# Chunked attention with a rational MLP: two weight pieces converted on GpSimd instead of ScalarE

## The chip, the cores and the metric

One Trainium2 chip, one core of it. The metric is the device time of one execution in microseconds (us). Before the change it is 855.72 us, the median of three runs.

## The reference

```python
scores = scale * np.matmul(q_c, k_c.transpose(0, 1, 2, 4, 3))      # chunks of 64
attn = np.exp(scores - max);  attn = attn / (sum + 1e-09)
x = (attn @ v_c) laid out as (4608, 512)
h = x @ w_in                                                     # (512, 2048)
P = a[0] + a[1] * h + a[2] * h2 + a[3] * h3
Q = 1.0 + np.abs(b[0]) * np.abs(h) + np.abs(b[1]) * h2
g = P / (Q + 1e-06)
return (g @ w_out).astype(np.float32)                            # (2048, 512)
```

The attention outputs of all heads become the 4608 rows of x. The weights arrive in double precision, the rest of the matrices in single precision.

## The kernel before

The 4608 rows are worked in 18 blocks of 256 rows. For each block the attention is made (scores, exponential, sums, the product with v) and split into a high and a low part, `xhi` and `xlo`. Then follow four stages of 512 columns of w_in each: the product `ph` with the weights' high and low parts (`wi_hi`, `wi_lo`), a chain of elementwise steps that makes the rational function (tiles A, B and C), and the product of its high and low parts (`ghi`, `glo`) with w_out (tile `wo`), gathered in `po`.

The first four blocks run while the weights still arrive. Their order is written out by hand in the string START; every word of it is one step, emitted to its engine at that point, and each engine works its own queue strictly in that order. A step is a letter and a number: a piece of the weights (0 to 15), or a stage of a block. What waits for what is found from the tiles that are read and written, including a wait for a buffer that is used again.

A piece of weights is a raw tile of 128 x 1024 double words. It goes through these steps:

- `w` loads it (a DMA from SP's queue; there are three raw buffers in turn).
- `o` or `oa` shifts its low word down: `o` on VectorE as an integer shift, `oa` on ScalarE as a scale and a bias on the upper half of the low word, converted to an integer (line 172).
- `s` scales the high word on ScalarE (line 176).
- `j` joins both words to a single-precision number on VectorE (line 180), and so needs `o`/`oa` and `s`.
- `h` rounds it to the high part on ScalarE (line 183), and so needs `j`.
- `d` or `dp` makes the low part as the difference, on VectorE or on GpSimd (line 190), needs `h`, and sets the raw buffer free.

Pieces 7 and 11 are pieces of w_in. Piece 7 is the second half of the third stage's columns, piece 11 the second half of the fourth's. In the rows their raw tiles are raw_364 (piece 7) and raw_493 (piece 11); raw_334 is piece 9, a piece of w_out.

Steps of the elementwise chain that stand near: `a`, `b`, `c` (lines 361, 365, 369) read `ph` on ScalarE and write A, B, C; `R` (line 404), `H` (line 396, `ghi`) and line 400 are VectorE's; `G` (line 409) makes `glo` from B and A on VectorE, `Gp` on GpSimd. A and B have two buffers each, so `a3` (the tile A_1_594) takes the buffer that A_0_329 leaves when `Gp0` (glo_0_608) has read it.

Of the kernel before, what the change touches and what calls it, by code (L numbers as in the profile page):

```python
# [13 lines left out]
AF = mybir.ActivationFunctionType  # L14
ALU = mybir.AluOpType
# [53 lines left out]
def tile_chunked_attention_rational_moe(  # L69
# [11 lines left out]
    nc = tc.nc  # L81
    cp = ctx.enter_context(tc.tile_pool(name="cp", bufs=1))
    p2 = ctx.enter_context(tc.tile_pool(name="p2", bufs=2))
# [15 lines left out]
    cst = cp.tile([P, 3], F32, tag="cst", name="cst")  # L99
    a0, a1, a2, a3 = (ab[:, i:i + 1] for i in range(4))  # L100
# [40 lines left out]
    raws, pls = {}, {}  # L141

    def grid(x, j):
        return x.rearrange("p (c f) -> p c f", c=2 if PIECES[j][0] else 4)

    def place(j, hi, lo):
        out, fq, k = PIECES[j]
        if out:
            c = slice(4 * fq + 2 * k, 4 * fq + 2 * k + 2)
            return hi[1][:, c, :], lo[1][:, c, :]  # L150
        f = slice(512 * fq + 256 * k, 512 * fq + 256 * k + 256)
        return hi[0][:, :, f], lo[0][:, :, f]
# [6 lines left out]
    def words(j):  # L159
        low, high = raws[j][:, :, 0], raws[j][:, :, 1]  # L160
        return low, high, high.bitcast(F32)

    def w_dest(j):
        return place(j, (wi_hi, wo_hi), (wi_lo, wo_lo))

    def w_low(j):
        low = words(j)[0]
        nc.vector.tensor_scalar(low, low, 29, None, ALU.logical_shift_right)

    def w_low_act(j):  # L170
        upper = raws[j].bitcast(mybir.dt.uint16).rearrange("p f (w h) -> p f w h", h=2)[:, :, 0, 1]
        nc.scalar.activation(words(j)[0], upper, AF.Identity, bias=cst[:, 2:3], scale=2.0 ** -13)

    def w_scale(j):
        val = words(j)[2]
# [12 lines left out]
    def w_diff(engine, j):  # L188
        hi, lo = w_dest(j)
        engine.tensor_sub(lo, grid(words(j)[2], j), hi.bitcast(F32))  # L190
        raws.pop(j)
# [610 lines left out]
    def fetch_behind(s):  # L802
# [3 lines left out]
    of_step = lambda f: lambda g: f(*steps[g])  # L806
    do = {
        "k": consts, "B": coefficients, "C": newton_coefficients, "D": newton_reciprocal, "q": queries, "v": load_v, "w": w_load,
        "o": w_low, "oa": w_low_act, "s": w_scale, "j": w_join, "h": w_hi,
        "d": lambda j: w_diff(nc.vector, j), "dp": lambda j: w_diff(nc.gpsimd, j), "r": w_rest, "l": w_lo,  # L810
        "S": att_s, "M": att_max, "U": att_sub, "E": att_exp, "n": att_rs, "Np": att_norm,
        "N": lambda n, u=None: att_norm(n, u, nc.vector), "m": lambda k: sums_of(*divmod(k, 14)), "t": fetch_behind,
# [176 lines left out]
```

## Time and profile before

| | before |
|---|---|
| median of 3 runs | 855.72 us (854.72 to 855.99) |
| profiled execution | 852.53 us, its span 850.7 us |
| TensorE (PE) busy | 822.4 us, 97% |
| VectorE (DVE) busy | 755.8 us, 89% |
| ScalarE (ACT) busy | 546.0 us, 64% |
| GpSimd (POOL) busy | 573.5 us, 67% |

The profiled execution is 3.2 us below the median; 1.8 us of its own time lie outside the span. The busy shares are means over the whole span, and they hide the first hundred microseconds, where TensorE is not full and the weights are converted.

### The profile page before, as it was taken

What the parts mean: (1) busy time and instruction counts of PE and PEld (TensorE: products, weight loads), DVE (VectorE), ACT (ScalarE), POOL (GpSimd) and SP (SyncE); (2) the same over time, 40 slices, a digit from 0 to 9 for tenths busy, and PEclk for the clock granted to TensorE, in tenths of its full rate; (3) what the DMA queues carried; (4) which work ended last, traced back from release to release, by engine and by line L of the source; (5) the groups of instructions that cost most, each with busy time, mean ns of one, the idle gap of its engine ahead of it and who ended that gap; (6) DMA issues with size and microseconds to landing.
All of it is one profiled execution on the core that took longest, in us unless ns stands there. A gap on an engine that the chain in (4) does not pass through costs nothing.

```text
span 850.7 us, 21032 instructions
## 1 busy us (share of the span) xinstructions
PE 822.4 (97%) x9054; PEld 813.0 (96%) x9054; DVE 755.8 (89%) x653; ACT 546.0 (64%) x550; POOL 573.5 (67%) x359
## 2 busy tenths in 40 slices
PE   2899899999999999999999999999999999999997
PEld 2799899999999999999999999999999999999997
DVE  6999999979888889998989898889888989888887
ACT  5899866657566666565666566666566666666553
POOL 1323475876777776777867777768776768777771
PEclk9999999999999999999999999999999999999999
DMA  8555332514757677777777776768777777776862
GB/s 330 182 186 220 106 119 76 198 51 159 263 154 223 211 233 235 236 248 230 246 242 248 224 252 212 243 215 253 229 248 236 245 243 229 235 229 189 277 214 73
DMA packets 144380, 179.63 MB, mean 211 GB/s; under 512 B 7584, under 2 KB 130464, under 8 KB 141216
## 3 DMA queue, kind: packets, MB, share of 16 engines
q1 hardware_dynamic: 144128, 178.03, 64.7%
q8 instruction: 71, 1.16, 0.5%
q10 hardware_dynamic: 160, 0.26, 0.1%
q14 instruction: 21, 0.17, 0.1%
HBM read 159.39 MB, written 18.87 MB: 210 GB/s over the span
## 4 chain that ended last, share of the span: by engine, by line
PE 86%; DVE 8%; DMA 3%; issue 2%; SPq 1%; ACT 0%; DVEq 0%; ACTq 0%
PE ph L355 40%; PE acc L624 18%; PE acd L624 13%; PE po L430 8%; PE psx L226 2%; PE pss L226 2%; PE pst L306 2%; DVE raw L180 1%; PE pe L668 1%; DMA wo<-t 1%; DMA raw<-in_w_in 1%; DVE C L385 1%; SPq L752 1%; DVE C L389 1%; DVE ghi L396 1%
## 5 line engine op out<-in xcount | busy, mean ns | idle before, releaser
L355 PE MATMUL ph<-xhi,wi_hi 128*128 128x256 f32 x1156 | 320.4, 278 | 2.2 <-DVE C L501 2.2
L355 PE MATMUL ph<-xhi,wi_lo 128*128 128x256 f32 x1152 | 319.6, 277 | 1.5 <-DVE wi_lo L190 1.5
L355 PE MATMUL ph<-xlo,wi_hi 128*128 128x256 f32 x1152 | 319.6, 277 | 0.0
L355 PEld LDWEIGHTS ph<-xhi,wi_hi 128*128 128x128 f32 x1156 | 218.1, 189 | 3.0 <-issue 2.3
L355 PEld LDWEIGHTS ph<-xhi,wi_lo 128*128 128x128 f32 x1152 | 217.4, 189 | 1.9 <-DVE wi_lo L190 1.9
L355 PEld LDWEIGHTS ph<-xlo,wi_hi 128*128 128x128 f32 x1152 | 217.6, 189 | 0.1
L553 POOL TENSOR_TENSOR slo<-B,shi 128x1024 fp32r<-128x1024 f32 x54 | 131.3, 2432 | 71.3 <-ACT shi L545 70.1
L463 ACT ACTIVATE U<-ph 128x1024 f32<-128x1024 f32 x64 | 65.8, 1030 | 159.9 <-PE ph L355 159.4
L472 DVE SCALAR_TENSOR_TENSOR U<-U,co 128x1024 f32<-128x1024 f32 x64 | 117.2, 1831 | 20.0 <-ACT U L463 20.0
L529 POOL TENSOR_TENSOR B<-C 128x512 f32<-128x512 f32 x54 | 81.6, 1511 | 67.6 <-DVE C L501 67.6
L493 DVE SCALAR_TENSOR_TENSOR U<-U,co,ph 128x1024 f32<-128x1024 f32 x64 | 80.5, 1258 | 42.6 <-ACT ph L489 42.5
L521 POOL TENSOR_TENSOR graw<-C,graw 128x768 fp32r<-128x768 f32 x54 | 100.0, 1852 | 0.7 <-ACT graw L516 0.7
L485 ACT ACTIVATE B<-U,cst,co 128x1024 f32<-128x1024 f32 x64 | 79.8, 1247 | 27.3 <-DVE U L472 26.2
L624 PE MATMUL acc<-wo,graw 128*128 128x256 f32 x648 | 92.6, 278 | 0.0
L489 ACT ACTIVATE ph<-B,co 128x1024 f32<-128x1024 f32 x64 | 71.6, 1119 | 19.1 <-DVE C L480 18.9
L480 DVE SCALAR_TENSOR_TENSOR C<-C,co,ph 128x1024 f32<-128x1024 f32 x64 | 81.8, 1277 | 1.7
L468 ACT ACTIVATE C<-ph,co 128x1024 f32<-128x1024 f32 x64 | 77.0, 1203 | 9.7 <-PE ph L355 6.0
L501 DVE SCALAR_TENSOR_TENSOR C<-C,co,ph 128x1024 f32<-128x1024 f32 x63 | 80.7, 1281 | 2.2
L624 PEld LDWEIGHTS acc<-wo,graw 128*128 128x128 f32 x648 | 81.7, 188 | 0.8
L497 DVE SCALAR_TENSOR_TENSOR ph<-U,ph 128x1024 f32<-128x1024 f32 x64 | 78.5, 1226 | 1.7
L534 POOL TENSOR_TENSOR B<-C,B 128x256 f32<-128x256 f32 x54 | 75.4, 1396 | 4.2
L476 DVE TENSOR_TENSOR C<-C,ph 128x1024 f32<-128x1024 f32 x64 | 77.5, 1211 | 0.2 <-ACT U L463 0.2
(118 smaller groups left out, 1577.8 us busy)
## 6 DMA issues: line engine op xcount, KB each, us to landing
wo<-t SPq DMA_DIRECT2D x106, 768.0 KB, 6.4
wo<-t SPq DMA_DIRECT2D x114, 256.0 KB, 3.4
out<-o SPq DMA_DIRECT2D x68, 128.0 KB, 6.0
raw<-in_w_in SPq DMA_DIRECT2D x8, 1024.0 KB, 5.1
raw<-in_w_out SPq DMA_DIRECT2D x8, 1024.0 KB, 4.8
v<-in_vP SPq DMA_DIRECT2D x24, 256.0 KB, 7.8
qk<-in_qT SPq DMA_DIRECT2D x44, 128.0 KB, 6.6
qk<-in_kT SPq DMA_DIRECT2D x44, 128.0 KB, 6.3
```

Of the source, the lines that this page charges most:

```text
L355: nc.tensor.matmul(ph[:, fi, t], w[:, cc, f], x[:, cc, t], start=(k == 0 and i == 0), stop=(k == len(mm) - 1),)
L472: nc.vector.scalar_tensor_tensor(U, U, c0, U, ALU.add, ALU.mult)
L476: nc.vector.tensor_mul(C, C, h)
L480: nc.vector.scalar_tensor_tensor(C, C, na1, h, ALU.add, ALU.mult)
L485: nc.scalar.activation(ch[key][2], ch[key][1], AF.Ln, bias=cst[:, 0:1], scale=lsc)
L493: nc.vector.scalar_tensor_tensor(V, V, kq, h, ALU.add, ALU.mult)
L497: nc.vector.scalar_tensor_tensor(h, V, 2.0, h, ALU.subtract, ALU.mult)
L501: nc.vector.scalar_tensor_tensor(C, C, na0, h, ALU.add, ALU.mult)
L521: nc.gpsimd.tensor_sub(lo, quads(ch[steps[g]][3])[:, :, 1:4, :], hi.bitcast(F32))
L529: nc.gpsimd.tensor_sub(S[:, 0:2], q[:, 0:1].to_broadcast([P, 2, 2, 128]), q[:, 1:3])
L553: nc.gpsimd.tensor_sub(lo, sbuf[g], hi.bitcast(F32))
L624: nc.tensor.matmul(acc[n][pair][:, bank, col + t.start:col + t.stop], stat, mov[:, t], start=start and k == 0, stop=stop and k == len(part ...
```

## The change

For the pieces 7 and 11 the step `oa` becomes `op`, a GpSimd instruction that multiplies and adds on the same upper halves, and `h` becomes `hp`, a copy on GpSimd. The words stand at the same places of START. No other step is changed.

```diff
-    "... F3:pa w11 s9 Q2 I2 s7 oa7 Z0 R0 p2 J2 P2 j7 z0 s11 g2 h7 F1:p1 f3 "
-    "H2 oa11 a3 d7 oa9 b3 j11 R2 h11 c3 j9 w6 Gp0 h9 Z2 G2 f1 d11 a1 f5:p0 ..."
+    "... F3:pa w11 s9 Q2 I2 s7 op7 Z0 R0 p2 J2 P2 j7 z0 s11 g2 hp7 F1:p1 f3 "
+    "H2 op11 a3 d7 oa9 b3 j11 R2 hp11 c3 j9 w6 Gp0 h9 Z2 G2 f1 d11 a1 f5:p0 ..."
...
+    def upper_half(j):
+        return raws[j].bitcast(mybir.dt.uint16).rearrange("p f (w h) -> p f w h", h=2)[:, :, 0, 1]
+
     def w_low_act(j):
-        upper = raws[j].bitcast(mybir.dt.uint16).rearrange("p f (w h) -> p f w h", h=2)[:, :, 0, 1]
-        nc.scalar.activation(words(j)[0], upper, AF.Identity, bias=cst[:, 2:3], scale=2.0 ** -13)
+        nc.scalar.activation(words(j)[0], upper_half(j), AF.Identity, bias=cst[:, 2:3], scale=2.0 ** -13)
+
+    def w_low_pool(j):
+        nc.gpsimd.tensor_scalar(words(j)[0], upper_half(j), 2.0 ** -13, -4095.5 / 8192.0, ALU.mult, ALU.add)
+
+    def w_hi_pool(j):
+        nc.gpsimd.tensor_copy(w_dest(j)[0], grid(words(j)[2], j))
```

How the queues stand. Line numbers of the changed kernel are 8 higher from line 182 on.

GpSimd's queue before, from the normalisation of block 1 and the low part of piece 8 on:

```order
L296 TENSOR_TENSOR e_258<-e_258,sm_253 128x2x8x64
L190 TENSOR_TENSOR wo<-raw_268,wo 128x1024
L409 TENSOR_TENSOR glo_0_608<-B_0_336,A_0_329 128x1024
L190 TENSOR_TENSOR wo<-raw_334,wo 128x1024
L190 TENSOR_TENSOR wi_lo<-raw_606,wi_hi 128x4x256
```

GpSimd's queue in the changed kernel, from the same place on:

```order
L304 TENSOR_TENSOR e_258<-e_258,sm_253 128x2x8x64
L198 TENSOR_TENSOR wo<-raw_268,wo 128x1024
L177 TENSOR_SCALAR raw_364<-raw_364 128x1024
L180 CAST wi_hi<-raw_364 128x4x256
L177 TENSOR_SCALAR raw_493<-raw_493 128x1024
L180 CAST wi_hi<-raw_493 128x4x256
L417 TENSOR_TENSOR glo_0_608<-B_0_336,A_0_329 128x1024
L198 TENSOR_TENSOR wo<-raw_334,wo 128x1024
```

The four new instructions (op7, hp7, op11, hp11) stand ahead of Gp0, which makes glo_0_608.

ScalarE's queue before, from the scaling of piece 7 on (the brackets name the engines or DMA queues that an instruction waits for):

```order
L176 ACTIVATE raw_364<-raw_364 128x1024 [waits DMAHW2_49,Pool_49]
L172 ACTIVATE raw_364<-raw_364,cst 128x1024
L381 ACTIVATE A_1_459<-A_1_459,cst 128x1024 [waits Activation_49]
L176 ACTIVATE raw_493<-raw_493 128x1024 [waits DMAHW3_49]
L183 CAST wi_hi<-raw_364 128x4x256 [waits DVE_49]
L172 ACTIVATE raw_493<-raw_493,cst 128x1024
L361 ACTIVATE A_1_594<-ph_1_467,ab 128x1024 [waits PE_49,Pool_49]
L172 ACTIVATE raw_334<-raw_334,cst 128x1024
L365 ACTIVATE B_1_598<-ph_1_467 128x1024
L183 CAST wi_hi<-raw_493 128x4x256 [waits DVE_49]
L369 ACTIVATE C_1_603<-ph_1_467,ab 128x1024
```

ScalarE's queue in the changed kernel, from the same place on:

```order
L184 ACTIVATE raw_364<-raw_364 128x1024 [waits DMAHW2_49,Pool_49]
L389 ACTIVATE A_1_459<-A_1_459,cst 128x1024 [waits Activation_49]
L184 ACTIVATE raw_493<-raw_493 128x1024 [waits DMAHW3_49]
L369 ACTIVATE A_1_594<-ph_1_467,ab 128x1024 [waits PE_49,Pool_49]
L174 ACTIVATE raw_334<-raw_334,cst 128x1024
L373 ACTIVATE B_1_598<-ph_1_467 128x1024 [waits DVE_49]
L377 ACTIVATE C_1_603<-ph_1_467,ab 128x1024
L191 CAST wo<-raw_334 128x1024 [waits DVE_49]
```

Four instructions are gone. The wait of A_1_594 (a3) for GpSimd is there before and after; in both programs it is the wait for Gp0. Behind it stands oa9, the shift of piece 9.

VectorE's queue in the changed kernel, from the join of piece 7 on:

```order
L188 SCALAR_TENSOR_TENSOR raw_364<-raw_364 128x1024 [waits DMAHW2_49,Activation_49,Pool_49]
L404 SCALAR_TENSOR_TENSOR ghi_1_539<-C_1_464,ab,A_1_459 128x1024 [waits DVE_49,Activation_49]
L408 SCALAR_TENSOR_TENSOR B_1_461<-B_1_461,ghi_1_539 128x1024 [waits DVE_49]
L198 TENSOR_TENSOR wi_lo<-raw_364,wi_hi 128x4x256 [waits Pool_49]
L188 SCALAR_TENSOR_TENSOR raw_493<-raw_493 128x1024 [waits DMAHW3_49,Activation_49,Pool_49]
L412 SCALAR_TENSOR_TENSOR B_1_461<-C_1_464,ab,B_1_461 128x1024 [waits DVE_49]
L188 SCALAR_TENSOR_TENSOR raw_334<-raw_334 128x1024 [waits DMAHW1_49,Activation_49]
L417 TENSOR_TENSOR glo_1_627<-B_1_461,A_1_459 128x1024 [waits DVE_49]
```

Its order is that of before (the DVE rows of the next section show it). The difference of piece 7 waited for ScalarE and now waits for GpSimd, and the join of piece 11 waits for GpSimd as well. The join of piece 9 (raw_334) waits for ScalarE's oa9, as before.

## Rows read from the trace of the kernel before

**Rows 1.** The page: the span, and the chain that ended last by engine.

```profile
span 850.7 us, 21032 instructions
...
PE 86%; DVE 8%; DMA 3%; issue 2%; SPq 1%; ACT 0%; DVEq 0%; ACTq 0%
```

**Rows 2.** Windows: busy us and instruction counts by engine, granted clock, DMA.

```profile
40.00:100.00 60.00, 56.36 (x529) 55.58 (x529) 59.58 (x53) 54.10 (x58) 23.78 (x9) 0.98 0.52 185
50.00:60.00 10.00, 10.00 (x91) 10.00 (x90) 9.93 (x9) 9.88 (x10) 1.97 (x1) 1.00 0.24 78
```

**Rows 3.** The chain in order of time near 98 us: start, us, what.

```profile
97.50 1.29 DVE C L501
...
98.93 4.59 PE ph L355 x24
...
105.33 2.72 PE ph L355 x24
```

**Rows 4.** Timeline of VectorE, 39 to 66 us: start, duration, instruction.

```profile
39.94 1.22 DVE L180 SCALAR_TENSOR_TENSOR raw<-raw 128x1024 int32<-128x1024 int32 x1
...
48.06 1.28 DVE L404 SCALAR_TENSOR_TENSOR B<-C,ab,B 128x1024 f32<-128x1024 f32 x1
...
51.71 1.35 DVE L180 SCALAR_TENSOR_TENSOR raw<-raw 128x1024 int32<-128x1024 int32 x1
52.98 1.27 DVE L396 SCALAR_TENSOR_TENSOR ghi<-C,ab,A 128x1024 fp32r<-128x1024 f32 x1
54.28 1.23 DVE L400 SCALAR_TENSOR_TENSOR B<-B,ghi 128x1024 f32<-128x1024 f32 x1
55.43 1.22 DVE L190 TENSOR_TENSOR wi_lo<-raw,wi_hi 128x1024 fp32r<-128x1024 f32 x1
56.56 1.22 DVE L180 SCALAR_TENSOR_TENSOR raw<-raw 128x1024 int32<-128x1024 int32 x1
57.70 1.28 DVE L404 SCALAR_TENSOR_TENSOR B<-C,ab,B 128x1024 f32<-128x1024 f32 x1
58.89 1.22 DVE L180 SCALAR_TENSOR_TENSOR raw<-raw 128x1024 int32<-128x1024 int32 x1
...
63.43 2.52 DVE L373 SCALAR_TENSOR_TENSOR B<-B,ab,A 128x1024 f32<-128x1024 f32 x1
```

**Rows 5.** Timeline of ScalarE, 50 to 58 us.

```profile
50.27 1.25 ACT L172 ACTIVATE raw<-raw,cst 128x1024 int32<-128x1024 uint16 x1
...
53.49 1.15 ACT L183 CAST wi_hi<-raw 128x1024 fp32r<-128x1024 f32 x1
...
55.94 1.12 ACT L361 ACTIVATE A<-ph,ab 128x1024 f32<-128x1024 f32 x1
56.96 1.26 ACT L172 ACTIVATE raw<-raw,cst 128x1024 int32<-128x1024 uint16 x1
```

**Rows 6.** Timeline of GpSimd, 40 to 65 us; brackets: idle before, and what ended it.

```profile
40.53 2.95 POOL L190 TENSOR_TENSOR wo<-raw,wo 128x1024 fp32r<-128x1024 f32 x1 [7.39 <-ACT wo L183]
49.49 2.48 POOL L409 TENSOR_TENSOR glo<-B,A 128x1024 fp32r<-128x1024 f32 x1 [6.00 <-DVE B L404]
62.41 2.46 POOL L190 TENSOR_TENSOR wo<-raw,wo 128x1024 fp32r<-128x1024 f32 x1 [10.44 <-ACT wo L183]
```

**Rows 7.** DMA issues between 43 and 44 us: count, size, us to landing.

```profile
raw<-in_w_in SPq DMA_DIRECT2D x1, 1024.0 KB, 4.8
```

**Rows 8.** GpSimd's groups by form: count, busy us, mean ns, idle before.

```profile
L190 POOL TENSOR_TENSOR wi_lo<-raw,wi_hi 128x1024 fp32r<-128x1024 f32 x2 | 4.9, 2443 | 4.7 <-ACT wi_hi L183 4.7
...
masks.py:199 POOL TENSOR_SCALAR_AFFINE_SELECT ident<-ident 128x128 f32<-128x128 f32 x1 | 0.3, 292 | 0.1
masks.py:197 POOL MEMSET ident<- 128x128 f32 x1 | 0.2, 204 | 0.3 <-POOLq L969 0.3
...
L777 POOL MEMSET cst<- 128x1 f32 x1 | 0.1, 98 | 0.0
```

**Rows 9.** Timeline of TensorE: its first wait for VectorE's last step.

```profile
98.93 0.36 PE L355 MATMUL ph<-xhi,wi_hi 128*128 128x256 f32 x1 [2.18 <-DVE C L501]
```

More of the change, by code (lines that the diff above doesn't have):

```diff
@@ L808, in tile_chunked_attention_rational_moe @@
         "k": consts, "B": coefficients, "C": newton_coefficients, "D": newton_reciprocal, "q": queries, "v": load_v, "w": w_load,
-        "o": w_low, "oa": w_low_act, "s": w_scale, "j": w_join, "h": w_hi,
+        "o": w_low, "oa": w_low_act, "op": w_low_pool, "hp": w_hi_pool, "s": w_scale, "j": w_join, "h": w_hi,
         "d": lambda j: w_diff(nc.vector, j), "dp": lambda j: w_diff(nc.gpsimd, j), "r": w_rest, "l": w_lo,
```

4 rows, old and new, of the table START are left out of this document.

## Prediction

> **What bounds the kernel now.** I read the page first. Its chain that ended last is TensorE for 86% of the 850.7 us and VectorE for 8%, about 68 us [rows 1]. A mean like that says nothing about a change at 50 us, so the next view was the chain in order of time. VectorE's last piece in it ends at 98.79 us, TensorE goes on at 98.93, and from there the chain stays with TensorE [rows 3]. TensorE itself stood idle for 2.18 us just then, and what released it was VectorE [rows 9]. So up to about 99 us VectorE sets the time, and behind it TensorE does. The windows say the same: from 40 to 100 us VectorE is busy for 59.58 of 60 us, TensorE for 56.36. Between 50 and 60 us ScalarE is nearly full too, 9.88 of 10, but VectorE with 9.93 is not waiting for it; GpSimd is busy for 1.97 [rows 2].
>
> What follows from this: four instructions fewer on ScalarE give nothing back by themselves, since VectorE's queue has no gap to close. A delay of VectorE before 99 us is passed on to the end in full, as TensorE cannot make it up later.
>
> **What goes and what comes.** ScalarE loses two shifts and two roundings, of 1.25 and 1.15 us in the rows of piece 7 [rows 5], some 4.8 us in all, none of it on the path. GpSimd gains four instructions of 128 x 1024. The trace has no GpSimd instruction with one such input, so I bound one. The two-input kind takes 2443 ns, an upper bound. A memset of 128 elements takes 204 ns and one of a single element 98, which is 0.83 ns an element and 0.95 us for 1024, a lower bound since it reads nothing. The nearest row reads one input and writes one output: the 128x128 select with 292 ns; (292 - 98)/127 is 1.53 ns an element, 1.66 us for 1024 [rows 8]. I take 1.6 us for each, o for a shift and h for a rounding, with 0.95 to 2.45 as bounds. The GPSIMD Engine Reference of the Trainium skill (section 3.1, Elementwise) gives about 1.8 cycles an element at best, by which I estimate 1.54 us; the delay below would be 9.3 instead of 9.5 us.
>
> **The new wait inside VectorE's queue.** The load of piece 7 is issued just after 43.5 us and lands 4.8 us later, near 48.4 [rows 7]. GpSimd is free by then: its low part of piece 8 ends at 43.48 [rows 6]. So op7 is done near 50 to 51.7, before VectorE comes to j7 at 51.71 [rows 4]. No cost there; j7 even loses the 0.13 us by which it was longer than the other joins (1.35 against 1.22), since GpSimd no longer runs glo_0_608 at that time.
>
> From j7 on VectorE's queue is j7, ghi, line 400, d7, j11. Its starts follow at 1.14, 1.30, 1.15 and 1.13 us [rows 4], so j11 would start at 51.71 + 4.72 = 56.43. But d7 now needs hp7, and j11 needs op11 behind hp7 on GpSimd. Can these two hide under VectorE's work? The trace has a row on that. VectorE's line 373 at 63.43 takes 2.52 us, where 1.27 is usual for such an instruction; GpSimd's instruction ended at 62.41 + 2.46 = 64.87, and VectorE's ended 1.08 us behind that [rows 4, 6]. The other way round, GpSimd's instruction at 40.53 took 2.95 us in place of 2.46, while VectorE's join ran until 41.16 [rows 4, 6]. So two SBUF inputs on VectorE and a GpSimd instruction do not run together. The State Buffer page of the Trainium skill (section Who interferes with whom) calls it an exclusive lock, held for the whole instruction, between VectorE with two SBUF inputs and any GpSimd instruction that reads SBUF; by that the delay is 9.5 us, and by overlap 5.3. The rows agree for two-input GpSimd instructions; no row has one with a single input. The instructions ghi, line 400, d7 and j11 have two SBUF inputs each, so I add both GpSimd times to the line: j11 starts at 56.43 + h + o, which is later than before (56.56) by h + o - 0.13 = 3.1 us. Which of the two gets in first does not matter for the sum.
>
> **The longer wait: Gp0 behind hp11.** GpSimd's queue is in order, and Gp0 now stands behind hp11, which needs j11. Gp0 ran at 49.49 before [rows 6]. ScalarE's a3 waits for Gp0 (it takes over its buffer), oa9 stands behind a3 on ScalarE, and VectorE's join of piece 9 needs oa9. Counted from the start of j11: VectorE's next instruction starts at 1.14 and holds the inputs until 1.14 + 1.28 = 2.42 (start and length of the row at 57.70). So hp11 ends at 2.42 + h. Gp0 takes 2.48: 4.90 + h. From a3 to oa9 are 56.96 - 55.94 = 1.02 us, and oa9 takes 1.26 [rows 5]: the join of piece 9 starts at 7.18 + h. Before it was 58.89 - 56.56 = 2.33 behind j11 [rows 4]. The added wait is 4.85 + h, 6.45 us, in which VectorE does nothing. Hand-overs of under 0.1 us each are left out.
>
> **The sum.** h + o - 0.13 + 4.85 + h = 4.72 + 2h + o, with 1.6 us for both 9.5 us. With 0.95 it is 7.6, with 2.45 it is 12.1. After the join of piece 9 each engine finds its queue as before, only later: c3, needed next from ScalarE, comes some 2 us behind oa9, while VectorE has three instructions of 1.2 us to do first. The loads that wait for the raw buffers of pieces 7 and 11 go out 3 and 9 us later, with VectorE. The 9.5 us then reach TensorE at 98.93 and the end. The span becomes 860.2 us, the profiled execution 852.53 + 9.5 = 862.0. That execution lies 3.2 us below the median of 855.72, so for the median I say 855.7 + 9.5 = 865.2 us.
>
> **Rivals.** (1) GpSimd with a single input runs beside VectorE. Then hp7 (52.93 to about 54.7) and op11 are done in time for d7 and j11, which gain 0.13. The hand-over from VectorE to GpSimd was 0.15 us (48.06 + 1.28 to 49.49) [rows 4, 6], so hp11 starts 1.22 + 0.15 behind j11, Gp0 ends at 3.85 + h, the join of piece 9 starts at 6.13 + h, and the delay is 3.67 + h = 5.3 us: 861.0. With h of 0.95 it is 4.6: 860.3. For it: no row has the single-input kind. Against it: the rows above show no kind that went beside. Chance 0.13.
>
> (2) Not slower: Gp0 is done before a3 needs it, at 55.94 [rows 5], and the 4.8 us taken from ScalarE count. With ScalarE ahead, GpSimd's low part of piece 9 at 62.41 would come earlier and no longer hold VectorE at 63.43 (1.25 us), and j7 gains 0.13: 855.7 - 1.4 = 854.3, within 0.2%. It decides if hp11 ends before 55.94 - 2.48 = 53.5. Against it: hp11 needs j11, four instructions behind j7 on VectorE, and j7 starts at 51.71; only a queue that lets Gp0 pass would do it. A kin of it is that the delay is hidden later, but VectorE had 0.42 us idle in all from 40 to 100 us [rows 2]. Both 0.05.
>
> (3) Longer GpSimd instructions: 16-bit input at a stride and the conversion to integers cost more than two float inputs, or TensorE comes back at a lower clock. The 24 matmuls from 98.93 took 4.59 us, those from 105.33 took 2.72 [rows 3], so a restart behind a wait can cost 1.9 us. With 3 us for o and h the delay is 13.7: 869.4, and 871.3 with such a restart. Chance 0.09.
>
> The forecast keeps 0.73.
>
> **Numbers.** Its own range is 855.7 + 7.6 to 855.7 + 12.1, 863.3 to 867.8. The range takes in rival 1 down to 860.3 less the 1 us by which runs of before lie apart, and upward 867.8 and a restart: 859.5 to 869.7. A difference under 0.2%, 1.7 us, is about what a measurement of this kernel cannot tell from none. Slower by more than that are the forecast and the rivals 1 and 3, 0.95; rival 2 is mostly no change, 0.03, and faster with 0.02.
>
> **What the next profile would show.** Gp0 starts behind hp11, past 60 us instead of at 49.49, and a3 on ScalarE shows an idle time of several us, released by GpSimd. VectorE shows two stalls: about 3 us between line 396 and the join of piece 11, partly as longer instructions, and about 6.5 us ahead of the join of piece 9. GpSimd's new instructions take between 0.95 and 2.45 us. VectorE's last piece in the chain ends near 108 instead of 98.79, and behind it all is as before. I am wrong if VectorE's instructions keep their length beside GpSimd's (rival 1), if a3 does not wait, or if the chain finds 9 us again between 68 and 99 us.

## The result and the profile after

The changed kernel takes 861.96 us, median of five runs (861.67 to 865.99); the kernel before, run beside it, 855.72 us, median of five (854.12 to 859.43). The ratio is 1.0068, 95% interval 1.0041 to 1.0095, which is 5.8 us more with 3.5 to 8.1. The medians lie 6.2 us apart. The change makes the kernel slower.

The page of the profile after, its span and its chain by engine, beside [rows 1]:

```profile
span 860.5 us, 21031 instructions
...
PE 83%; DVE 8%; DMA 3%; issue 2%; POOL 2%; ACT 1%; SPq 0%; DVEq 0%; POOLq 0%; ACTq 0%
```

GpSimd and ScalarE were hardly in the chain before; now they hold 2% and 1%. Where, the chain in order of time says (start, us, what):

```profile
60.58 2.08 POOL wi_hi L180
62.66 2.41 POOL glo L417
65.10 1.11 ACT A L369
66.21 1.09 ACT raw L174
67.33 0.04 DVE raw L188
...
105.78 1.29 DVE C L509
107.07 0.14 issue
107.21 4.32 PE ph L363 x24
```

It goes from GpSimd's rounding of piece 11 through Gp0 (line 417) to ScalarE's a3 (line 369) and oa9 (line 174), and to the join of piece 9 on VectorE (line 188). Before, VectorE held this stretch alone. Behind it nothing is new: from the join of piece 9 to the end of VectorE's last step are 107.07 - 67.33 = 39.74 us, and before 98.79 - 58.89 = 39.90 us [rows 3, 4].

The windows (span of the window; busy us and instruction counts of PE, weight loads, DVE, ACT, POOL; granted clock of TensorE; DMA share; GB/s), beside [rows 2]:

```profile
40.00:100.00 60.00, 55.43 (x515) 54.84 (x509) 54.11 (x46) 44.52 (x49) 29.59 (x12) 0.90 0.43 158
50.00:60.00 10.00, 10.00 (x90) 10.00 (x89) 9.93 (x8) 4.28 (x5) 5.60 (x3) 1.00 0.14 57
60.00:70.00 10.00, 5.43 (x47) 5.23 (x46) 4.38 (x5) 4.90 (x5) 4.49 (x2) 0.95 0.28 105
65.00:70.00 5.00, 0.43 (x3) 0.26 (x2) 2.67 (x3) 4.90 (x5) 0.07 (x1) 0.91 0.00 0
70.00:75.00 5.00, 5.00 (x24) 5.00 (x25) 5.00 (x4) 5.00 (x6) 2.73 (x1) 0.50 0.65 215
```

VectorE, full before, is busy for 54.11 of 60 us; the loss lies between 60 and 70 us, where it works for 4.38 of 10. From 50 to 60 us it looks as full as before, 9.93 us, but with 8 instructions in place of 9: a wait inside an instruction counts as busy. Its timeline (start, us, instruction; brackets: idle before, and what ended it), beside [rows 4]:

```profile
52.88 1.22 DVE L188 SCALAR_TENSOR_TENSOR raw<-raw 128x1024 int32<-128x1024 int32 x1
54.02 1.28 DVE L404 SCALAR_TENSOR_TENSOR ghi<-C,ab,A 128x1024 fp32r<-128x1024 f32 x1
55.33 2.02 DVE L408 SCALAR_TENSOR_TENSOR B<-B,ghi 128x1024 f32<-128x1024 f32 x1
57.27 2.11 DVE L198 TENSOR_TENSOR wi_lo<-raw,wi_hi 128x1024 fp32r<-128x1024 f32 x1
59.30 1.22 DVE L188 SCALAR_TENSOR_TENSOR raw<-raw 128x1024 int32<-128x1024 int32 x1
60.44 1.27 DVE L412 SCALAR_TENSOR_TENSOR B<-C,ab,B 128x1024 f32<-128x1024 f32 x1
67.33 1.23 DVE L188 SCALAR_TENSOR_TENSOR raw<-raw 128x1024 int32<-128x1024 int32 x1 [5.62 <-ACT raw L174]
```

The two stalls can be read off. Lines 408 and 198 take 2.02 and 2.11 us in place of 1.23 and 1.22: 0.79 and 0.89 us inside the instruction. Then VectorE stands still for 5.62 us before the join of piece 9. GpSimd's timeline, beside [rows 6]:

```profile
49.53 2.00 POOL L177 TENSOR_SCALAR raw<-raw 128x1024 int32<-128x1024 uint16 x1 [4.89 <-DMA raw<-in_w_in]
54.16 2.10 POOL L180 CAST wi_hi<-raw 128x1024 fp32r<-128x1024 f32 x1 [2.63 <-DVE raw L188]
56.34 1.97 POOL L177 TENSOR_SCALAR raw<-raw 128x1024 int32<-128x1024 uint16 x1
60.58 2.08 POOL L180 CAST wi_hi<-raw 128x1024 fp32r<-128x1024 f32 x1 [2.27 <-DVE raw L188]
62.63 2.44 POOL L417 TENSOR_TENSOR glo<-B,A 128x1024 fp32r<-128x1024 f32 x1
```

Gp0 starts at 62.63 instead of 49.49, behind the rounding of piece 11. The new instructions show some 2 us each, but about half of that is waiting: the rounding at 60.58 ends at 62.66, and VectorE's line 412, which held the inputs, ended at 60.44 + 1.27 = 61.71. From there it took 0.95 us. On ScalarE, a3 shows the wait for Gp0, and oa9 follows it:

```profile
65.10 1.11 ACT L369 ACTIVATE A<-ph,ab 128x1024 f32<-128x1024 f32 x1 [10.82 <-POOL glo L417]
66.11 1.18 ACT L174 ACTIVATE raw<-raw,cst 128x1024 int32<-128x1024 uint16 x1
```

How much later is the kernel behind this stretch? A mark that every kernel has is VectorE's first row maximum of a block. The marks of blocks 1 and 2, before (line 262) and after (line 270):

```profile
23.59 1.23 DVE L262 TENSOR_REDUCE sm<-pss 128x16 f32<-128x1024 f32 x1 [0.40 <-PE pss L226]
77.00 1.22 DVE L262 TENSOR_REDUCE sm<-pss 128x16 f32<-128x1024 f32 x1
...
24.76 1.22 DVE L270 TENSOR_REDUCE sm<-pss 128x16 f32<-128x1024 f32 x1 [0.40 <-PE pss L234]
85.26 1.22 DVE L270 TENSOR_REDUCE sm<-pss 128x16 f32<-128x1024 f32 x1
```

The 1.17 us ahead of block 1 are not the change's: VectorE's first shift waits for the first piece of w_in, and starts at 9.23 instead of 8.06. So between the two marks the change costs 8.26 - 1.17 = 7.09 us. I call this the local cost below. In block 3 the shift is 125.83 - 117.55 = 8.28 us, the same. Further back the two profiled executions drift apart by another 1 to 2 us and together again, and end at 860.5 against 850.7, which a pair of single executions can't put down to the change. Part of the drift shows on TensorE, in the chain after:

```profile
130.43 8.48 PE ph L363 x72
```

That is 117.8 ns a matmul, where before 72 of them take 8.16 us at 122.28, 113.3 ns each. The granted clock is 1.00 in both from 120 to 800 us. Later blocks mostly take the same 44.42 us in both kernels.

### The profile page after: what moved, and what is told of

It is laid out like the page before. It is cut to its first block, busy times and chain, and to the rows that moved or that the text cites. A ratio compares the mean times of both kernels' runs of the same rounds, so it can differ in the third digit from the quotient of the medians.

```text
span 860.5 us, 21031 instructions
## 1 busy us (share of the span) xinstructions
PE 827.2 (96%) x9054; PEld 817.5 (95%) x9054; DVE 760.5 (88%) x653; ACT 541.0 (63%) x546; POOL 582.9 (68%) x363
## 4 chain that ended last, share of the span: by engine, by line
PE 83%; DVE 8%; DMA 3%; issue 2%; POOL 2%; ACT 1%; SPq 0%; DVEq 0%; POOLq 0%; ACTq 0%
PE ph L363 39%; PE acc L632 17%; PE acd L632 13%; PE po L438 6%; PE psx L234 2%; DMA wo<-t 2%; PE pss L234 2%; PE pst L314 2%; DMA raw<-in_w_in 1%; DVE U L480 1%; PE pe L676 1%; DVE raw L188 1%; DVE C L393 1%; DVE B L381 1%; DVE sm L297 1%
## 5 line engine op out<-in xcount | busy, mean ns | idle before, releaser
L480 DVE SCALAR_TENSOR_TENSOR U<-U,co 128x1024 f32<-128x1024 f32 x64 | 120.1, 1876 | 18.5 <-ACT U L471 18.4
```

The lines of the kernel that those rows point to most:

```text
L480: nc.vector.scalar_tensor_tensor(U, U, c0, U, ALU.add, ALU.mult)
```

## The experiments

All were timed in five rounds beside runs of the kernel before on the same chip. The local cost of each is the shift of block 2's mark less that of block 1's, read from one profiled execution. This table has all results; the profiles follow one by one.

| kernel | median, of before | ratio (95%) | as us | local cost, us |
|---|---|---|---|---|
| the change | 861.96, 855.72 | 1.0068 (1.0041 to 1.0095) | 5.8 | 7.09 |
| e1_gp0_early | 860.37, 857.94 | 1.0027 (1.0006 to 1.0048) | 2.3 | 3.78 |
| e2_shift_only | 859.31, 857.94 | 1.0020 (0.9996 to 1.0045) | 1.7 | 2.22 |
| e3_round_only | 864.26, 857.94 | 1.0082 (1.0050 to 1.0113) | 7.0 | 7.16 |
| e4_wait_only | 886.14, 857.94 | 1.0328 (1.0293 to 1.0364) | 28.1 | 6.22 |
| e5_wait_only | 860.65, 856.79 | 1.0057 (1.0032 to 1.0082) | 4.9 | 5.70 |
| e6_six_copies | 861.24, 856.79 | 1.0048 (1.0023 to 1.0073) | 4.1 | 5.19 |
| e7_six_memsets | 856.92, 856.79 | 1.0002 (0.9977 to 1.0027) | 0.2 | -0.15 |
| e8_apart | 853.83, 856.79 | 0.9976 (0.9951 to 1.0002) | -2.1 | -1.72 |

In the profiled executions of five kernels, part of the local cost lies ahead of the join of piece 7 and is not due to what they change. VectorE waits for ScalarE there, for 0.29 us in e1, 0.73 in e3, 0.76 in e4, 0.39 in e5 and 0.75 in e6. In e3, for one, ScalarE itself had first waited 1.75 us for TensorE's `ph`. The profile of before has no such wait.

**Gp0 put ahead.** The changed kernel with Gp0 moved to a place before the first rounding, so that a3 need not wait for hp11:

```diff
-    "... j7 z0 s11 g2 hp7 F1:p1 f3 "
-    "H2 op11 a3 d7 oa9 b3 j11 R2 hp11 c3 j9 w6 Gp0 h9 ..."
+    "... j7 z0 s11 g2 Gp0 hp7 F1:p1 f3 "
+    "H2 op11 a3 d7 oa9 b3 j11 R2 hp11 c3 j9 w6 h9 ..."
```

> The changed kernel with the step Gp0 put ahead of hp7 in GpSimd's queue; nothing else differs. Queue theory (most of the loss is a3 waiting for Gp0 behind hp11): the idle time of ScalarE ahead of a3 that GpSimd ends (10.8 us in the changed kernel) falls under 1.5 us and VectorE's 5.6 us of idle time ahead of the join of piece 9 is gone; what stays is the shared inputs, 1.2 us for j7 behind Gp0, 1.6 for hp7 and op11, 0.95 for hp11: 2.5 to 4 us above before, about 859. Rival (the GpSimd instructions themselves hold VectorE up): the loss stays at 6 us, about 862.

Two rows of VectorE and one of ScalarE from its timelines:

```profile
48.67 2.21 DVE L412 SCALAR_TENSOR_TENSOR B<-C,ab,B 128x1024 f32<-128x1024 f32 x1
...
62.13 2.13 DVE L188 SCALAR_TENSOR_TENSOR raw<-raw 128x1024 int32<-128x1024 int32 x1
...
57.73 1.12 ACT L369 ACTIVATE A<-ph,ab 128x1024 f32<-128x1024 f32 x1 [4.04 <-PE ph L363]
```

The wait is gone: a3 starts at 57.73, released by TensorE and not by GpSimd, and the join of piece 9 at 62.13 has no idle time ahead of it. What is left is the sharing. The join itself takes 2.13 us beside the rounding of piece 11, line 412 takes 2.21 beside the first shift, and from the join of piece 7 (53.24) to that of piece 11 (59.80) are 6.56 us, before 4.85 [rows 4]. Together 0.91 + 0.93 + 1.71 = 3.55 of the local 3.78 us. The sum is near the one expected, but not all of its parts: Gp0 does not hold the join of piece 7 longer than before (1.33 us, before 1.35), and the wait of line 412 beside the first shift was not foreseen. Nearly half of the local cost goes by moving one word.

**The shifts alone**, the rounding left on ScalarE (`hp7` and `hp11` back to `h7` and `h11`):

```diff
-    "... s11 g2 hp7 F1:p1 f3 H2 op11 a3 d7 oa9 b3 j11 R2 hp11 c3 ..."
+    "... s11 g2 h7 F1:p1 f3 H2 op11 a3 d7 oa9 b3 j11 R2 h11 c3 ..."
```

> Only the two shifts on GpSimd, the rounding on ScalarE as before. Queue theory: Gp0 stands behind op11, which needs nothing of VectorE, so Gp0 ends near 54 to 55.5 and a3 hardly waits; Gp0 now meets VectorE's j7 and ghi and costs up to 2.4 us: 0.5 to 2.5 us above before, 856.2 to 858.2. Rival: half of the GpSimd work, half of the loss, 3 us, 858.7, and a3 as late as in the changed kernel.

Two rows of GpSimd and one of VectorE:

```profile
52.17 1.15 POOL L177 TENSOR_SCALAR raw<-raw 128x1024 int32<-128x1024 uint16 x1 [0.63 <-DVE C L393]
53.41 3.31 POOL L417 TENSOR_TENSOR glo<-B,A 128x1024 fp32r<-128x1024 f32 x1
...
54.33 3.47 DVE L404 SCALAR_TENSOR_TENSOR ghi<-C,ab,A 128x1024 fp32r<-128x1024 f32 x1
```

Here the shift of piece 11 runs beside an instruction of VectorE that reads one of its inputs from `ph`, TensorE's output, and takes 1.15 us: the price of a shift alone. Gp0 starts at 53.41, before at 49.49, and now meets `ghi`, which takes 3.47 us in place of 1.28. That is 2.19 of the 2.22 us of the local cost. So the shifts themselves hardly make VectorE wait here (the join of piece 7 takes 1.51 us, before 1.35); they push Gp0 onto another instruction with which it can't share. The timed 1.7 us have an interval that just takes in none. From the join of piece 11 to that of piece 9 are 62.45 - 60.11 = 2.34 us, as before (2.33).

**The rounding alone**, the shifts left on ScalarE:

```diff
-    "... s7 op7 Z0 R0 p2 J2 P2 j7 z0 s11 g2 hp7 F1:p1 f3 H2 op11 a3 ..."
+    "... s7 oa7 Z0 R0 p2 J2 P2 j7 z0 s11 g2 hp7 F1:p1 f3 H2 oa11 a3 ..."
```

> Only the two roundings on GpSimd, the shifts on ScalarE as before. Queue theory: Gp0 stays behind hp11 and so behind the join of piece 11; the wait ahead of the join of piece 9 stays at 5 to 6 us and the shared inputs cost 0.9 less than in the changed kernel: 5.5 to 7 us above before, 861 to 862.5. Rival: half of the GpSimd work, 3 us, 858.7.

One row each of GpSimd, ScalarE and VectorE:

```profile
62.55 2.44 POOL L417 TENSOR_TENSOR glo<-B,A 128x1024 fp32r<-128x1024 f32 x1
...
65.02 1.12 ACT L369 ACTIVATE A<-ph,ab 128x1024 f32<-128x1024 f32 x1 [8.19 <-POOL glo L417]
...
67.24 1.23 DVE L188 SCALAR_TENSOR_TENSOR raw<-raw 128x1024 int32<-128x1024 int32 x1 [5.62 <-ACT raw L174]
```

The rounding alone costs as much as the full change, 7.16 us locally, with the same 5.62 us ahead of the join of piece 9. The 0.9 us that leaving the shifts on ScalarE was expected to save are there: line 198 takes 1.22 us in place of 2.11. But they do not show in the total, since in this execution VectorE lost 0.73 us ahead of the join of piece 7: 0.29 for ScalarE's step `b` and 0.44 for the shift of piece 7 on ScalarE.

**The wait alone, first try.** The kernel before, with one instruction more: GpSimd copies one element of the joined piece 11 ahead of Gp0, so that Gp0 stands behind j11 with no conversion to do. The copied element is read by nobody.

```diff
-    "H2 oa11 a3 d7 oa9 b3 j11 R2 h11 c3 j9 w6 Gp0 ..."
+    "H2 oa11 a3 d7 oa9 b3 j11 R2 x11 h11 c3 j9 w6 Gp0 ..."
+    look = cp.tile([P, 1], F32, tag="look", name="look")
...
+    def w_look(j):
+        nc.gpsimd.tensor_copy(look, words(j)[2][:, 0:1])
```

> The kernel before with one GpSimd copy of a single element per partition, read from the joined piece 11, just ahead of Gp0; shifts and roundings stay on ScalarE. This has the queue's wait without the work. Queue theory: Gp0 starts near 59 instead of 49.5, a3 near 61.6, the join of piece 9 near 63.9 instead of 58.9: 4.5 to 5 us above before, 860.5. Rival: under 0.3 us, 855.7 to 856.

It came out 28 us slower, far from anything expected. The local cost is 6.22 us, so the rest is elsewhere, and two marks far behind show where (block starts on VectorE):

```profile
268.20 1.23 DVE L266 TENSOR_REDUCE sm<-pss 128x16 f32<-128x1024 f32 x1
314.38 1.23 DVE L266 TENSOR_REDUCE sm<-pss 128x16 f32<-128x1024 f32 x1
```

A block takes 46.18 us there, and before 302.43 - 258.01 = 44.42. Every later block is some 1.7 us longer, though not one instruction of them differs. The page shows on which engine:

```profile
PE 852.8 (97%) x9054; PEld 843.2 (95%) x9054; DVE 742.5 (84%) x653; ACT 542.9 (61%) x550; POOL 577.6 (65%) x360
```

TensorE is busy for 852.8 us with the same 9054 matmuls that take 822.4 before; in the later blocks 48 in a row take 5.68 us instead of 5.44 (118.3 ns each instead of 113.3), at a granted clock of 1.00. What does differ is the place of the tiles: the new tile has 4 bytes per partition and moves all tiles made after it. The run can't be used for the wait, and was made again without the new tile.

**The wait alone, second try.** The same copy, written into a filler tile of the kernel that is already there and never read:

```diff
-    cp.tile([P, 48], F32, tag="gap", name="wo_gap")
+    look = cp.tile([P, 48], F32, tag="gap", name="wo_gap")
...
+    def w_look(j):
+        nc.gpsimd.tensor_copy(look[:, 0:1], words(j)[2][:, 0:1])
```

> The wait without the work again: the kernel before with one GpSimd copy of a single element per partition, read from the joined piece 11, ahead of Gp0, now written into the gap that the kernel already has, so that no tile moves (in the run before, a new tile moved all later ones). Queue theory: VectorE's idle time ahead of the join of piece 9 is 4 to 5 us, the steady blocks take the time that they take before, 5 to 6.5 us above before, about 861. Rival (the shared inputs are the loss): under 1.3 us, since one element per partition holds nothing up.

Two rows of GpSimd, two of VectorE:

```profile
59.35 1.18 POOL L175 COPY wo_gap<-raw 128x1 f32<-128x1 f32 x1 [14.73 <-DVE raw L183]
60.48 2.44 POOL L412 TENSOR_TENSOR glo<-B,A 128x1024 fp32r<-128x1024 f32 x1
...
65.18 1.23 DVE L183 SCALAR_TENSOR_TENSOR raw<-raw 128x1024 int32<-128x1024 int32 x1 [4.71 <-ACT raw L172]
...
69.73 3.07 DVE L376 SCALAR_TENSOR_TENSOR B<-B,ab,A 128x1024 f32<-128x1024 f32 x1
```

With no conversion at all, the order of the queue alone costs 4.9 us timed and 5.70 locally. From the join of piece 11 (58.06) to that of piece 9 are 7.12 us, before 2.33: 4.79 us. The prediction's term for this wait, without the rounding, was 4.85. Line 376 takes 3.07 us in place of 2.52, another 0.55, as GpSimd's low part of piece 9 now meets it differently. The rest of the local cost is the wait of 0.39 us ahead of the join of piece 7.

**The sharing alone.** The kernel before with six single-input GpSimd copies of 128 x 1024 behind Gp0, where nothing waits for them, and once with six memsets in the same place. Both write a part of `wo` that later gets its weights, so the result doesn't change; one memset at the start fills the source.

```diff
-    "... c3 j9 w6 Gp0 h9 Z2 ..."
+    "... c3 j9 w6 Gp0 x0 h9 Z2 ..."
...
+    spare = [wo[:, 0, c:c + 2, :].bitcast(F32) for c in (12, 14)]
+    nc.gpsimd.memset(spare[1], 0.0)
...
+        for _ in range(6):
+            nc.gpsimd.tensor_copy(wo[:, 0, 12:14, :], spare[1])
```

With the memsets the last line is `nc.gpsimd.memset(spare[0], 0.0)`.

> The kernel before with six GpSimd copies of 128 x 1024, one input each, behind Gp0, into a part of wo that is written over later; nothing waits for them. If a single-input instruction and two SBUF inputs on VectorE exclude each other, VectorE's instructions between 52 and 65 us grow by about 0.95 us for each copy that meets one: 4 to 5.7 us above before, 860 to 861.5. If they run beside each other: under 0.3 us, 856.

> The same with six memsets of the same size, which read nothing from SBUF. If only reading shares the inputs: VectorE's instructions keep their length, under 0.5 us, 856. If every GpSimd instruction shares them: as the copies, 4 to 5.5 us.

GpSimd and two rows of VectorE with the copies:

```profile
51.92 10.94 POOL L787 CAST wo<-wo 128x1024 fp32r<-128x1024 f32 x6
...
53.96 2.06 DVE L396 SCALAR_TENSOR_TENSOR ghi<-C,ab,A 128x1024 fp32r<-128x1024 f32 x1
...
57.92 2.06 DVE L190 TENSOR_TENSOR wi_lo<-raw,wi_hi 128x1024 fp32r<-128x1024 f32 x1
```

And with the memsets:

```profile
52.91 6.05 POOL L787 MEMSET wo<- 128x1024 f32 x6
...
53.97 1.27 DVE L396 SCALAR_TENSOR_TENSOR ghi<-C,ab,A 128x1024 fp32r<-128x1024 f32 x1
...
56.42 1.22 DVE L190 TENSOR_TENSOR wi_lo<-raw,wi_hi 128x1024 fp32r<-128x1024 f32 x1
```

With copies, VectorE's instructions grow from 1.22 to 1.28 us to about 2.06, and the two engines take turns: from the join of piece 7 to that of piece 9 VectorE needs 63.86 - 52.27 = 11.59 us in place of 58.89 - 51.71 = 7.18. That is 4.41 us for six copies, 0.74 each, less than the 0.95 expected; the rest of the local 5.19 us is the 0.75 us ahead of the join of piece 7. With memsets no instruction of VectorE grows, and the time is that of before. So a GpSimd instruction that reads one input holds up VectorE's two-input instructions, and one that only writes does not. The SBUF — State Buffer page of the Trainium skill (section Who interferes with whom) says just this: two SBUF inputs on VectorE contend with a GpSimd instruction that reads SBUF, not with one that only writes it. The runs agree, with 0.74 us a copy and nothing for a memset.

**Apart.** A try at the reverse: give GpSimd only what it can hide. The kernel before, with the shift of piece 8 (on VectorE until now) on GpSimd, behind the normalisation of block 1, and with line 373 (`Q3`) put behind `P3`, whose instructions read `ph`, so that these stand beside GpSimd's low part of piece 9.

```diff
-    "... s8 o8 Q0 ...  p3 Q3 s6 q2 y2 oa6 b1 P3 dp9 ..."
+    "... s8 op8 Q0 ...  p3 P3 s6 q2 y2 oa6 b1 Q3 dp9 ..."
```

> The kernel before with VectorE's line 373 of the fourth chain behind its line 389, so that GpSimd's low part of piece 9 falls beside instructions that read PSUM, and with the shift of piece 8 on GpSimd in place of VectorE's. If the shared inputs are what holds VectorE up: line 373 takes 1.3 to 1.6 us in place of 2.52, and 0.6 us of VectorE's shift goes: 0.8 to 1.6 us below before, 854.1 to 854.9, which may not stand out of the measurement. Rival: nothing, 855.7.

One row of GpSimd and two of VectorE:

```profile
34.08 2.03 POOL L176 TENSOR_SCALAR raw<-raw 128x1024 int32<-128x1024 uint16 x1
...
35.00 1.21 DVE L389 TENSOR_TENSOR C<-C,ph 128x1024 f32<-128x1024 f32 x1
...
64.99 1.28 DVE L377 SCALAR_TENSOR_TENSOR B<-B,ab,A 128x1024 f32<-128x1024 f32 x1
```

The instruction that took 2.52 us beside GpSimd [rows 4] takes 1.28, since the instructions ahead of it that now run beside GpSimd read `ph`, and keep their length. VectorE's shift of 0.68 us is gone, and the shift on GpSimd holds nobody (the instruction beside it reads `ph`, 1.21 us). Locally this gains 1.72 us, and the median is 853.83 us, the lowest of all kernels here; the ratio of 0.9976 has an interval that just takes in 1.

## Why the prediction was right, point by point

**The bound.** VectorE sets the time up to about 99 us, and a delay there is passed on: shown. The local cost of every kernel but e4, from -1.72 to 7.16 us, lies in the interval of its timed difference. Whether it is passed on in full is less sure: for the six kernels in the table that are slower, e4 aside, the timed difference is smaller than the local cost each time, by 0.2 to 1.5 us. In e1, e3, e5 and e6, 0.3 to 0.8 us of the local cost are the wait ahead of the join of piece 7, which is not due to what they change. Single executions differ by more, among other things in the pace of TensorE (113.3 or 117.8 ns a matmul), so this stays open. That ScalarE's four instructions give nothing back was read from one execution. In e5, with the shift of piece 7 still on ScalarE, ScalarE waited 1.27 us for `ph` and VectorE then 0.39 us for that shift; in the changed kernel ScalarE waited 1.25 us for the same `ph`, and VectorE for nothing there. So some 0.4 us may come back in such an execution, which no run tests by itself.

**Gp0 behind hp11.** The chain a3, oa9, join of piece 9 was the prediction's largest term, 4.85 + h. The after trace has each of its links, e5 makes the wait with no conversion (4.79 us at the join), e1 takes it away and keeps both conversions, and only the rounding brings it (e3, not e2). The mechanism is shown. In the full change the term measured 5.70 us: from the join of piece 11 at 59.30 to that of piece 9 at 67.33 are 8.03, before 2.33. Predicted were 6.45.

**The inputs that VectorE and GpSimd share.** h + o - 0.13, predicted 3.1 us with 1.6 for each. That single-input instructions on GpSimd do not run beside VectorE's two-input ones was taken over from two-input rows, and e6 against e7 shows that it holds. The term measured 1.57 us: 59.30 - 52.88 = 6.42 from join to join, in place of 4.85. It is the 0.79 and 0.89 us by which lines 408 and 198 grew, less the 0.13 that the join of piece 7 lost, as it was said to.

**What was off: the size of h and o.** I took 1.6 us, from the 128x128 select, the nearest row by its kind [rows 8]. The lower bound, the memset, was nearer: VectorE lost 0.79 to a rounding and 0.89 to a shift, a rounding took 0.95 us after it was let in, and a shift that nothing held up took 1.15 (e2) and 1.11 us (e1). The wait inside VectorE is shorter than the GpSimd instruction itself, so even the lower bound of 0.95 was a little high for that term. With the measured values the sum is 0.79 + 0.89 - 0.13 + 4.85 + 0.95 = 7.35, against 7.27 by the two stalls and 7.09 at block 2's mark. That puts 865.2 us down to 863.0; the measured 861.96 lies 1.1 lower, inside what the interval leaves open. That the profiled execution took 862.30 us, where 862.0 was forecast, and its span 860.5 against 860.2, is luck: besides the 7.1 us these hold the 1.17 us ahead of block 1 and the drift behind block 3. The lower end of the stated range does not follow from its words either: 860.3 less 1 is 859.3, not 859.5. From the GPSIMD Engine Reference of the Trainium skill (section 3.1, Elementwise) I had estimated 1.54 us for such an instruction; no run here shows so much where nothing held the instruction up, and the 1.11 to 1.15 us measured decide.

**The rivals.** (1) That single-input instructions run beside VectorE is refuted by e6 and by lines 408 and 198. Its time of 861.0 us lies 1.0 below the median, the forecast with the measured h and o 1.0 above it: the time alone would not have told them apart. (2) Gp0 done before a3 needs it: refuted, a3 shows GpSimd as its releaser. With Gp0 put ahead (e1) the kernel is still slower. (3) Longer instructions: they are shorter than forecast. Its other half, TensorE's clock behind the wait, did happen, but at no cost that shows (below). (4) One that was not named is the place of the tiles, to which some 22 of e4's 28 us go (below). It plays no part in the change, whose later blocks mostly take the same 44.42 us as before.

## What to carry to other kernels

Before an instruction is moved to an engine with idle time, look at what stands behind it in that engine's queue, and who waits for that: here 4 instructions on an engine that was busy for 1.97 of 10 us cost 6 us, the greater part through one instruction that was only queued behind them. Look also at what runs beside it: VectorE's two-input instructions lose 0.7 to 0.9 us to each 128x1024 copy or shift on GpSimd, those that read `ph` lose nothing (1.21 us beside the shift in e8), so the place for such work is beside the latter. And work taken from an engine that is hardly waited for gives hardly anything back, however busy it is (ScalarE, 9.88 of 10 us busy).

## What the runs showed of the hardware that was not expected

- **The place of a tile.** One new tile of 4 bytes made each later block 1.7 us longer (e4, ratio 1.0328), with the same instructions, though the new copy runs only once, near 59 us. The same copy into a tile that was there cost 1.0057. The loss is in the pace of TensorE's matmuls, 118.3 ns instead of 113.3. The runs don't show what in the placement matters.
- **Two paces at one clock.** The same matmuls took 113.3 or 117.8 ns each in different stretches, at a granted clock of 1.00: in the changed kernel 117.8 ns from 130 to 139 us, and 113.3 before. Other profiled executions show such stretches elsewhere. The runs don't show what sets the pace.
- **One element waits as long as a thousand.** The copy of a single element took 1.18 us on GpSimd (e5): it started at 59.35, and VectorE's two-input instruction ran until 59.20 + 1.28 = 60.48. It ended 0.05 us behind that.
- **A restart at the lower clock that cost nothing.** In the changed kernel TensorE waited 4.57 us for VectorE's `glo`:

```profile
69.74 1.65 PE L438 MATMUL po<-wo,glo 128*128 128x256 f32 x6 [4.57 <-DVE glo L417]
```

It was busy for 0.43 of the 5 us from 65 to 70 us; from 70 to 75 its granted clock was 0.50, the lower of its levels (1.2 of 2.4 GHz), and it finished 24 matmuls in that window. VectorE, which sets the pace there, needed 39.74 us from the join to its last step, as before.
